# Attention of the last two batches: fp32 scores in 64x32 tiles, p transposed by VectorE, values in 64x64 tiles

## The chip, the cores and the metric

One core of one Trainium2 chip runs the program. The metric is device time in microseconds (us) of one execution, the median of three: 1250.9 us (1250.06 to 1251.99). The profile shown here is of one more execution of the same program, which took 1250.11 us; the profiled span inside it is 1248.3 us.

Engines: PE is TensorE's matmul (PEld its weight load), DVE is VectorE, ACT is ScalarE, POOL is GpSimd, and SP issues the DMAs.

## The reference, cut to what matters

```python
# q, k, v: (4 batches, 8 heads, 1152, 64), fp32
q_pool = q.reshape(B, H, S // 2, 2, D).mean(axis=3)             # 576 queries
scores = scale * np.matmul(q_pool, k.transpose(0, 1, 3, 2))     # 576 x 1152
scores = scores - np.max(scores, axis=-1, keepdims=True)
attn = np.exp(scores)
attn = attn / (np.sum(attn, axis=-1, keepdims=True) + 1e-09)
x = np.matmul(attn, v)                 # heads side by side: 2304 tokens x 512
h = x @ w_in                           # 512 -> 2048
x = np.maximum(0.01 * h, h) @ w_out    # 2048 -> 512
h = np.maximum(np.maximum(x @ w1, x @ w2), x @ w3)   # 512 -> 768, three times
out = h @ w_out2                       # 768 -> 512
```

The two heads of a pair are worked on together: 4 batches of 4 pairs, numbered n = 0 to 15. The third batch begins with pair 8.

## The kernel before

**Two streams.** `attention()` walks over the 16 pairs, and `experts(b)` over the two MoE layers of one batch of tokens. MoE of batch b runs beside the attention of batch b+1; MoE of the last batch runs alone, together with a leftover (`Rest`) of 64 tokens of every batch, 256 in all. Beside the attention of pairs 8 to 15 stands thus the MoE of the second and third batches.

**MoE.** A product (`product`, L706) is 12 matmuls of 128x512 into one PSUM bank, in fp32r (each operand is split in a high and a low part, three matmuls per product of parts). ScalarE or VectorE then take the bank's content away. The last layer (tiles `o`) has 18 matmuls of 128x256 per bank.

**Attention.** A pair goes through two phases, ph 0 with 320 queries and ph 1 with 256. For each query tile:
- `scores` (L318): 128 queries of one head by 1152 keys. Queries and keys are split in a high and a low half that lie on the 128 partitions, so six fp32r matmuls of 128x384 (two per bank, three banks) do a tile; the tile "m" holds the last 64 queries of both heads and takes twelve. That is 36 + 24 = 60 matmuls for a pair. The three banks are one tile `s`, held once: the next tile's matmuls wait until it has been read.
- VectorE takes the row maximum `mx` of the whole tile (L362), ScalarE the exponential into `p` with the row sum beside it (L363).
- `normalise` (L368): from pair 8 on VectorE adds 1e-9, takes the reciprocal and multiplies all of `p` with it (L377, L378, L382).
- `probs_t` and `probs_m` (L407, L418): TensorE transposes `p` in blocks of 128x128 into `pst` and `psf`, 72 + 9 blocks for a pair; ScalarE and VectorE copy them to `pt` (L416, L423).
- `values` (L429): 18 fp32 products a phase, with 64 columns of v as weights and 320 or 256 queries streamed, the two heads in two halves of the columns of the array. `evac` (L452) writes the two parts of x.
- `prep_q`, `prep_k`: transposes of q and k for the next pair, and their split in two halves by ScalarE and VectorE; the halves are sent to the other partitions by DMA (L288).

**PSUM.** From pair 4 on `s` has three banks, `pv` one, and the other four are shared by MoE's products and all transposes (`bank`, L136).

**Order of the work.** The two generators are interleaved by slots (`S_AT`, `RATIO`, L1173), which gives an order to start from. Then `plan()` rebuilds the whole program as a graph, gives each instruction a cost and plays the five engines forward, always taking the step that can start first (ties by how late it may be done); three rounds at most. The order that comes out is fixed for each engine. So an engine never overtakes: if the instruction at its front waits, all behind it wait too.

Of the kernel before, what the change touches and what calls it, by code (L numbers as in the profile page):

```python
# [23 lines left out]
def kernel(  # L24
# [32 lines left out]
    SC = 3  # L57
# [11 lines left out]
    slots = {}  # L69

# [17 lines left out]
    kt_p = Pool("kt", 1)  # L88
    vs_p = Pool("vs", 2)
    p_p = Pool("p", 9)  # L90
    st_p = Pool("st", 12)
    rr_p = Pool("rr", 6)
    m_p = Pool("mb", 1)
    xf_p = Pool("xf", 1)
    pt_p = Pool("pt", 2)
# [8 lines left out]
    ps_v = Pool("ps_v", 1, space=bass.MemoryType.PSUM)  # L104
    ps_m = Pool("ps_m", 2, space=bass.MemoryType.PSUM)
    psum = ExitStack()
    ctx.callback(psum.close)
    ps_5 = Pool("ps_5", 1, psum, space=bass.MemoryType.PSUM)
    s_pair = [ps_5.tile([128, 2, 512], F32, name=f"s2{i}") for i in range(2)]
    s_mid = ps_5.tile([128, 512], F32, name="s1")  # L110

    ident = const.tile([128, 128], F32, name="ident")
    rb = [const.tile([128, w], F32, name=f"rb{w}") for w in (X0, T - X0)]
    qt = {}
    for j in range(2):
        for part in range(2):
            qt[j, part] = const.tile([128, T + 64], F32R, name=f"q{j}{part}")
# [15 lines left out]
    ps_w = {}  # L133
    turn = [0]

    def bank(name, spare=False):  # L136
        if spare:
            return ps_v.tile([128, 512], F32, tag="v", name=name)
        turn[0] += 1
        pool = ps_w["m"] if ps_w and turn[0] % 2 == 0 else ps_m  # L140
        return pool.tile([128, 512], F32, tag="m", name=name)

    def wide_scores():
        if not ps_w:
            psum.close()
            ps_s = Pool("ps_s", 1, space=bass.MemoryType.PSUM)
            ps_w["s"] = ps_s.tile([128, SC, 512], F32, name="s")
            ps_w["m"] = Pool("ps_n", 2, space=bass.MemoryType.PSUM)
        return ps_w["s"]
# [320 lines left out]

    GATE = 0
# [11 lines left out]
    def attention():  # L483
        npair = B * NP
# [31 lines left out]
        for u, (n, ph) in enumerate(phases):  # L516
# [11 lines left out]
            if ph == 0 and n + 1 < npair:  # L528
# [6 lines left out]
                if n + 2 < npair:  # L535
                    at(max(0, s0 + (-2 if early else 15)), 0, load_pair, n + 2)
                if n + 1 >= NP:
                    at(s0 + 8, 0, load_v, n + 1)
            if n < FREE:
# [46 lines left out]
        yield from follow()  # L586
        assert not todo
# [152 lines left out]
    class Rest:  # L740
        n = TR_

        def __init__(self):
            def parts(name):
                t = p_p.tile([128, SC, SN], F32, tag="p", name=name).rearrange("p a b -> p (a b)")
                t = t[:, 0:1024].bitcast(F32R).rearrange("p (i a t) -> p i a t", i=2, a=2)
# [5 lines left out]
            acc = p_p.tile([128, SC, SN], F32, tag="p", name="accrest").rearrange("p a b -> p (a b)")  # L752
# [96 lines left out]
    def plan():  # L849
# [38 lines left out]
        for i in todo:  # L888
# [4 lines left out]
            if key is not None and last and last["unit"] == (key, out):  # L893
# [32 lines left out]
        wide_at = next(n for n, node in enumerate(nodes) if node["out"] and slots[node["out"]][0][0] == "ps_s")  # L926
        for n, node in enumerate(nodes):
            busy = late = move = 0.0
            for i in node["ins"]:
# [4 lines left out]
                if e == "PE":  # L934
                    if kind == "pv":
                        one = cols / 1.2
                    elif kind in ("pst", "psf", "psk", "psr"):
# [14 lines left out]
                elif e == "Activation":  # L952
                    late = 185 + 0.8 * cols + 190 * (len(i.outs) > 1) + 180 * ((kind[0] == "q") or kind == "kspare")
                    busy = late - 105
                elif e == "DVE":
# [3 lines left out]
                    slow = psum or op in ("TensorTensor", "TensorReduce") or kind == "wmant"  # L959
                    late = max(155, 110 + (1.13 if slow else 0.62) * cols + 190 * (kind[0] == "q"))  # L960
                    busy = late - 80
                else:
                    late = 45 + 2.44 * cols
                    busy = late - 45
# [4 lines left out]
            node["busy"], node["late"], node["move"] = busy, late, move  # L969

# [26 lines left out]
        wide = [n for t in users if slots[t][0][0] == "ps_5" for n in users[t]]  # L997
# [7 lines left out]
        def forward(prio):  # L1005
            heads = {g: 0 for g in queue}
            rooms = {g: [(0.0, "")] * slots[q[0]][1] for g, q in queue.items()}
            narrow, narrow_at = len(wide), 0.0
# [10 lines left out]
            values_last = False  # L1019
            for _ in range(count):  # L1020
                best = None
                for e in ENGINES:
                    for n in pool[e]:
                        t = max(ready[n], free[e])
                        if nodes[n]["shut"]:
                            t = max(t, shut)
                        for x in need[n]:
                            group = slots[x][0]
                            if queue[group][heads[group]] != x or not rooms[group]:
                                break  # L1030
                            t = max(t, rooms[group][0][0])
# [179 lines left out]
```

## Time and profile before

| what | value |
|---|---|
| time, median of 3 | 1250.9 us (1250.06 to 1251.99) |
| profiled execution | 1250.11 us, its span 1248.3 us |
| PE busy | 1220.3 us, 98% of the span |
| DVE / ACT / POOL busy | 635.2 / 631.6 / 295.2 us |
| mean granted TensorE clock | 0.996 of full speed |
| second and third batch of MoE beside the attention of pairs 8 to 15 | 460 us to 995 us |
| last batch of MoE, alone | 995 us to the end |

"Busy" is the time in which an engine has an instruction running. PE's instructions overlap: a matmul's record begins when it is issued and ends when its last result has arrived, so the mean duration of one is longer than the pace at which they follow each other. A pace is read from the timeline, as the distance of two starts divided by the number of matmuls between them.

An fp32 product with both operands as they are (here those of `values`) appears in the trace as two matmul records, each with its own weight load; 18 products are 36 records. A transpose and an fp32r matmul are one record each.

### The profile page before, as it was taken

What the parts mean: (1) busy time and instruction counts of PE and PEld (TensorE: products, weight loads), DVE (VectorE), ACT (ScalarE), POOL (GpSimd) and SP (SyncE); (2) the same over time, 40 slices, a digit from 0 to 9 for tenths busy, and PEclk for the clock granted to TensorE, in tenths of its full rate; (3) what the DMA queues carried; (4) which work ended last, traced back from release to release, by engine and by line L of the source; (5) the groups of instructions that cost most, each with busy time, mean ns of one, the idle gap of its engine ahead of it and who ended that gap; (6) DMA issues with size and microseconds to landing.
All of it is one profiled execution on the core that took longest, in us unless ns stands there. A gap on an engine that the chain in (4) does not pass through costs nothing.

```text
span 1248.3 us, 19152 instructions
## 1 busy us (share of the span) xinstructions
PE 1220.3 (98%) x7392; PEld 1006.8 (81%) x7392; DVE 635.2 (51%) x1100; ACT 631.6 (51%) x1251; POOL 295.2 (24%) x265
## 2 busy tenths in 40 slices
PE   6999999999999999999999999999999999999998
PEld 5676677888778887878888897878878798888888
DVE  6877657766776745465655435565645111222110
ACT  6887878676776645453645435453634222112111
POOL 1111144444543412120211101120200022223110
PEclk9999999999999999999999999999999999999999
DMA  5522168676877655363534455363433363333433
GB/s 161 139 74 75 35 223 266 221 231 240 268 252 230 213 166 159 110 175 102 165 130 140 153 184 146 109 190 102 140 122 112 110 206 122 132 120 109 143 110 111
DMA packets 86902, 193.29 MB, mean 155 GB/s; under 512 B 11292, under 2 KB 41756, under 8 KB 86812
## 3 DMA queue, kind: packets, MB, share of 16 engines
q1 hardware_dynamic: 86812, 192.08, 49.1%
q8 instruction: 58, 0.95, 0.3%
q14 instruction: 32, 0.26, 0.1%
HBM read 146.80 MB, written 35.13 MB: 146 GB/s over the span
## 4 chain that ended last, share of the span: by engine, by line
PE 91%; ACT 4%; DVE 3%; issue 1%; DMA 1%; DVEq 0%; ACTq 0%
PE m L123 48%; PE s L123 13%; PE pv L123 11%; PE pst L123 10%; PE o L123 6%; PE psf L123 1%; PE psq L123 1%; PE psk L123 1%; ACT q L280 1%; DVE q L284 1%; DVE kt L233 1%; ACT kt L230 0%; ACT p L358 0%; ACT p L355 0%; ACT p L363 0%
## 5 line engine op out<-in xcount | busy, mean ns | idle before, releaser
L123 PE MATMUL m<-x,w 128*128 128x512 f32 x1224 | 307.2, 396 | 0.3 <-ACT ptw L416 0.3
L123 PEld LDWEIGHTS m<-x,w 128*128 128x128 f32 x1224 | 223.0, 188 | 42.7 <-issue 1.0
L362 DVE TENSOR_REDUCE mx<-s 128x1 f32<-128x1152 f32 x108 | 146.5, 1356 | 105.4 <-PE s L123 105.1
L123 PE MATMUL s<-kt,q 128*128 128x384 f32 x832 | 184.4, 354 | 5.5 <-ACT p L355 2.4
L363 ACT ACTIVATE p<-s,mx 128x1152 f32<-128x1152 f32 x108 | 132.1, 1223 | 93.7 <-DVE mx L362 93.2
L787 POOL TENSOR_TENSOR g<-t,g 128x512 fp32r<-128x512 f32 x64 | 84.1, 1315 | 382.8 <-DVE g L786 382.8
L123 PE MATMUL pst<-ident,p 128*128 128x128 f32 x1080 | 166.4, 276 | 5.1 <-ACT pt L416 1.1
L123 PEld LDWEIGHTS pst<-ident,p 128*128 128x128 f32 x1080 | 129.0, 140 | 49.5 <-issue 11.8
L416 ACT COPY pt<-pst 128x512 f32<-128x512 f32 x216 | 124.6, 587 | 82.6 <-PE pst L123 78.9
L123 PEld LDWEIGHTS s<-kt,q 128*128 128x128 f32 x832 | 143.4, 192 | 14.3 <-ACT p L355 3.1
L123 PE MATMUL m<-g,w 128*128 128x512 f32 x576 | 147.7, 397 | 0.1
L123 PEld LDWEIGHTS m<-g,w 128*128 128x128 f32 x576 | 104.3, 188 | 18.6 <-ACT ptw L416 0.3
L785 ACT ACTIVATE t<-m 128x512 f32<-128x512 f32 x80 | 44.4, 555 | 127.7 <-PE m L123 127.1
L123 PE MATMUL m<-x,wsplit 128*128 128x512 f32 x408 | 106.9, 401 | 0.0
L123 PE MATMUL pv<-pt,v 128*64 128x256 f32 (+1 forms) x720 | 96.7, 407 | 0.0
L665 POOL TENSOR_TENSOR wsplit<-wraw,wsplit 128x512 fp32r<-128x512 f32 x56 | 74.9, 1341 | 83.8 <-ACT wsplit L664 67.0
L815 DVE TENSOR_TENSOR t<-m,t 128x512 f32<-128x512 f32 (+1 forms) x60 | 38.2, 636 | 99.6 <-PE m L123 99.3
L123 PEld LDWEIGHTS m<-x,wsplit 128*128 128x128 f32 x408 | 73.6, 188 | 14.0 <-issue 1.3
L786 DVE CAST g<-t 128x512 fp32r<-128x512 f32 x64 | 27.9, 436 | 107.3 <-ACT t L785 106.9
L123 PEld LDWEIGHTS pv<-pt,v 128*64 128x64 f32 x720 | 48.5, 137 | 37.4 <-issue 8.8
L725 POOL TENSOR_TENSOR y<-t,y 128x512 fp32r<-128x512 f32 x24 | 32.6, 1357 | 187.5 <-ACT y L724 187.5
L382 DVE TENSOR_SCALAR p<-p,sums 128x1152 f32<-128x1152 f32 x76 | 67.2, 885 | 2.6
(120 smaller groups left out, 1577.5 us busy)
## 6 DMA issues: line engine op xcount, KB each, us to landing
w<-w SPq DMA_DIRECT2D x168, 512.0 KB, 3.4
w<-wsplit SPq DMA_DIRECT2D x56, 512.0 KB, 6.5
wraw<-in_moe_w_out_dram SPq DMA_DIRECT2D x22, 512.0 KB, 6.0
wraw<-in_moe_w_dram SPq DMA_DIRECT2D x18, 512.0 KB, 5.1
kraw<-in_k_dram SPq DMA_DIRECT2D x15, 576.0 KB, 9.6
qraw<-in_q_dram SPq DMA_DIRECT2D x15, 576.0 KB
q<-q SPq DMA_DIRECT2D x52, 160.0 KB, 5.2
wraw<-in_moe_w_in_dram SPq DMA_DIRECT2D x16, 512.0 KB, 4.3
```

What stands on the lines that cost most here:

```text
L123: mm = f(*args, **kwargs)
L233: nc.vector.tensor_tensor(out=t[lo, c], in0=src, in1=t[hi, c], op=ALU.subtract)
L362: nc.vector.tensor_reduce(out=mx[:, 0:1], in_=ps[:, :, 0:SN], axis=AX.XY, op=ALU.max, negate=True)
L363: nc.scalar.activation(out=p[2], in_=ps[:, :, 0:SN], func=ACTF.Exp, bias=mx[:, 0:1], accum_out=rs[:, i:i + 1])
L382: nc.vector.tensor_scalar(out=x, in0=x, scalar1=rs[:, i:i + 1], scalar2=None, op0=ALU.mult)
L416: nc.scalar.copy(out=dst, in_=ps.rearrange("p (j c) -> p j c", j=2))
L665: nc.gpsimd.tensor_tensor(out=t[:, 1], in0=r, in1=t[:, 0], op=ALU.subtract)
L725: nc.gpsimd.tensor_tensor(out=t[:, 1], in0=src, in1=t[:, 0], op=ALU.subtract)
L785: nc.scalar.activation(out=t, in_=ps[:, 0:k.n], func=ACTF.Prelu, alpha=0.01)
L786: nc.vector.tensor_copy(out=gt[:, 0], in_=t)
L787: nc.gpsimd.tensor_tensor(out=gt[:, 1], in0=t, in1=gt[:, 0], op=ALU.subtract)
L815: nc.vector.tensor_tensor(out=t, in0=ps[:, 0:k.n], in1=t, op=ALU.max)
```

## The change

Pairs 0 to 7 are left as they were. For pairs 8 to 15 `attention2()` takes over from `attention()`:

- **PSUM.** When the second batch's attention is done, its pools are closed. Attention gets six banks of its own: four for `s` (one tile, held once) and one each for `a` and `b`. MoE keeps two (`ps_m`), where it shared four before.
- **Scores.** `prep2` puts the 64 components of head 0 on partitions 0 to 63 and those of head 1 on 64 to 127, unsplit fp32; no halves, no DMA. `scores2` does 64 queries of both heads in 16 fp32 products of 288 keys, each with 64 rows and 32 columns of the array: two row halves (heads) by four column quarters. A quarter holds 32 queries and half of the keys, so a query's keys lie on two partition groups. A pair has 5 + 4 such tiles.
- **Maximum.** One reduction over the whole tile, then `meet_halves`: four copies of 32 partitions that lay the other half's maximum beside each partition's own, and a minimum (the values are negated).
- **Exponential** in two instructions of 576 elements, one for each head.
- **Transpose.** VectorE's transpose of 32x32 blocks, one instruction for the whole of `p` (128x1152), into `pt`.
- **Values.** `values2` does 72 products a phase with 64 rows and 64 columns of the array (two key halves by two heads); `join` adds the two halves of the row sums by one small product, GpSimd lays their reciprocals out (`rd`), and two products with a constant 0.5 spread them over the partitions. `evac2` multiplies with them, so that `p` itself is not normalised.
- The planner knows the new forms, and some of its other costs are changed (GpSimd's and VectorE's), so the order of the first two batches can move as well.

```diff
+    def split_array():
+        if not sec:
+            full.close()
+            for name, bufs in (("kt", 2), ("vs", 1), ("p", 3), ("rr", 3), ("r", 1), ("pt", 1), ("c", 1), ("rz", 1)):
+                sec[name] = Pool(f"{name}2", bufs)
+            sec["s"] = Pool("ps_q", 1, space=bass.MemoryType.PSUM)
+            sec["v"] = Pool("ps_w", 1, space=bass.MemoryType.PSUM)
...
-        pool = ps_w["m"] if ps_w and turn[0] % 2 == 0 else ps_m
+        pool = ps_w["m"] if ps_w and turn[0] % 2 == 0 and not sec else ps_m
...
+    def other(x, name):
+        return sec["v"].tile([128, 512], F32, tag=x, name=name)
...
-        npair = B * NP
+        npair = NB * NP
...
+    def prep2(n, j):
+        if j == 0:
+            kts2[n] = sec["kt"].tile([128, S], F32, tag="k", name="kt")
+            qts[n] = sec["kt"].tile([128, T], F32, tag="q", name="q")
+        qr = raws[n][0][:, j].rearrange("p c r d -> p (c r d)")
+        kr = raws[n][1][:, j].rearrange("p c d -> p (c d)")
+        r = slice(64 * j, 64 * j + 64)
+        ni = QC // 2
+        w = ni * QP
+        psq, psk = other("a", "psq"), other("b", "psk")
+        for i in range(ni):
+            transpose(psq[:, i * QP:(i + 1) * QP], qr[:, (4 * i + 1) * D:(4 * i + 3) * D], ident[:QP, :QP])
+        transpose(psq[:64, w:w + 128], kr[:, (KT - 1) * D:KT * D], sec["pairs"])
+        for e in range(2):
+            nc.scalar.mul(
+                out=qts[n][r].rearrange("p (t i e) -> p e i t", e=2, i=ni)[:, e],
+                in_=psq[64 * e:64 * e + 64, 0:w].rearrange("p (i t) -> p i t", t=QP),
+                mul=scale,
+            )
+        nc.scalar.copy(
+            out=keys(kts2[n], r, KT - 1, KT),
+            in_=psq[:64, w:w + 128].rearrange("d (m a i) -> d m a i", m=1, a=4),
+        )
+        unit[0] += 1
+        for i in range(4):
+            transpose(psk[:, i * 128:(i + 1) * 128], kr[:, i * 128:(i + 1) * 128], sec["pairs"])
+        unit[0] += 1
+        for e in range(2):
+            nc.scalar.copy(
+                out=keys(kts2[n], r, e, KT - 1, 2),
+                in_=psk[64 * e:64 * e + 64].rearrange("d (m a i) -> d m a i", m=4, a=4),
+            )
...
+    def meet_halves(st, z):
+        for c in range(4):
+            d = c + 1 - 2 * (c % 2)
+            nc.vector.tensor_copy(out=st[32 * c:32 * c + 32, :, 1], in_=st[32 * d:32 * d + 32, :, 0])
+        nc.vector.tensor_reduce(out=z, in_=st, axis=AX.X, op=ALU.min)
+
+    def scores2(n, ph, i):
+        if i == 0:
+            sums2[n, ph] = sec["rr"].tile([128, 2, tiles2(ph)], F32, tag=f"rr{ph}", name="sums")
+            ptl2[n, ph] = flipped(ph)
+        rs, pt = sums2[n, ph], ptl2[n, ph]
+        whole = sec["s"].tile([128, 4, 512], F32, tag="s", name="s")
+        ps = whole
+        every = ps[:, :, 0:KQ].rearrange("p (h x) k -> p h x k", h=2)
+        ps = [ps[:, 0:2], ps[:, 2:4]]
+        c0 = X0 * ph + QB * i
+        unit[0] += 1
+        joint.add(unit[0])
+        for x in range(2):
+            for a in range(4):
+                for h in range(2):
+                    r = slice(64 * h, 64 * h + 64)
+                    c = c0 + 32 * (a // 2)
+                    k0 = KQ * (2 * (a % 2) + x)
+                    matmul(
+                        out=ps[h][32 * a:32 * a + 32, x, 0:KQ],
+                        lhsT=qts[n][r, c:c + 32],
+                        rhs=kts2[n][r, k0:k0 + KQ],
+                        start=True,
+                        stop=True,
+                    )
+        p = sec["p"].tile([128, 4, KQ], F32, tag="p", name="p")
+        st = whole[:, 0, KQ:KQ + 4].rearrange("p (h s) -> p h s", h=2)
+        z = st_p.tile([128, 2], F32, tag="z", name="z")
+        nc.vector.tensor_reduce(out=st[:, :, 0], in_=every, axis=AX.XY, op=ALU.max, negate=True)
+        meet_halves(st, z)
+        for h in range(2):
+            nc.scalar.activation(
+                out=p[:, 2 * h:2 * h + 2], in_=ps[h][:, :, 0:KQ], func=ACTF.Exp, bias=z[:, h:h + 1],
+                accum_out=rs[:, h, i:i + 1],
+            )
+        nc.vector.transpose(
+            out=pt[:, :, i].rearrange("p m h j -> p h m j"),
+            in_=p.rearrange("p (h x) (m i) -> p h (x m) i", h=2, m=KT),
+        )
...
+    def values2(n, ph):
+        w = width2(ph)
+        rs = sums2.pop((n, ph)).rearrange("p h u -> p (h u)")
+        pt = ptl2.pop((n, ph))
+        nu = rs.shape[1]
+        ps = other("b", "psr")
+        unit[0] += 1
+        matmul(out=ps[:, 0:nu], lhsT=sec["join"], rhs=rs, start=True, stop=True)
+        nc.vector.tensor_scalar(out=rs, in0=ps[:, 0:nu], scalar1=1e-9, scalar2=None, op0=ALU.add)
+        nc.vector.reciprocal(out=rs, in_=rs)
+        rd = sec["r"].tile([128, 2 * X0], F32, tag="r", name="rd")[:, 0:2 * w]
+        nj = 2 * w // nu
+        nc.gpsimd.tensor_tensor(
+            out=rd.rearrange("p (u j) -> p u j", j=nj),
+            in0=rs.unsqueeze(2).to_broadcast([128, nu, nj]),
+            in1=sec["fold"].unsqueeze(1).to_broadcast([128, nu, nj]),
+            op=ALU.mult,
+        )
+        unit[0] += 1
+        joint.add(unit[0])
+        two = [other(x, "pw") for x in "ab"]
+        pv2[0] = [two[g][:, 0:w // 2] for g in range(2)]
+        for m in range(2 * KT):
+            for j in range(2):
+                for g in range(2):
+                    r = slice(64 * g, 64 * g + 64)
+                    mm = matmul(
+                        out=pv2[0][g][64 * j:64 * j + 64],
+                        lhsT=vss[n][r, j, m],
+                        rhs=pt[r, m, :, j],
+                        start=(m == 0),
+                        stop=(m == 2 * KT - 1),
+                    )
+        unit[0] += 1
+        pv2[1] = two[0][:, X0 // 2:X0 // 2 + w]
+        for j in range(2):
+            matmul(
+                out=pv2[1][64 * j:64 * j + 64, 0:w],
+                lhsT=sec["half"],
+                rhs=rd[:, j * w:(j + 1) * w],
+                start=True,
+                stop=True,
+            )
+        unit[0] += 1
...
+        nc.scalar.copy(out=rz[:, 0:w], in_=pv2[1][:, 0:w])
+        for g in range(2):
+            a, b_ = [y[:, 0:w].rearrange("p (t g j) -> p g t j", g=2, j=32)[:, g] for y in (xf, rz)]
+            nc.vector.tensor_tensor(out=a, in0=pv2[0][g].rearrange("p (t j) -> p t j", j=32), in1=b_, op=ALU.mult)
+        nc.scalar.copy(out=t[:, 0, c], in_=xf[:, 0:w])
+        nc.gpsimd.tensor_tensor(out=t[:, 1, c], in0=xf[:, 0:w], in1=t[:, 0, c], op=ALU.subtract)
...
+    S2 = ((0, 2, 4, 6, 7), (0, 2, 4, 6))
+    RATIO2 = 1.7
...
+                for i in range(tiles2(nxt[1])):
+                    at(s0 + S2[nxt[1]][i], S_COST, scores2, *nxt, i)
...
+        def both():
+            yield from attention()
+            yield from attention2()
```

The order of the instructions, engine by engine, shows what the planner makes of it. On PE, beside the MoE of the second batch (`m<-x`, `m<-g` are MoE's products), a stretch of the kernel before:

```order
L123 MATMUL m<-g,w 128x512 x18
L123 MATMUL pst<-ident,p 128x128 x4
L123 MATMUL psf<-ident,p 128x128 x3
L123 MATMUL s<-kt_4951,q_123 128x384
L123 MATMUL s<-kt_4951,q_124 128x384
L123 MATMUL s<-kt_4951,q_123 128x384
L123 MATMUL s<-kt_4951,q_124 128x384
L123 MATMUL s<-kt_4951,q_123 128x384
L123 MATMUL s<-kt_4951,q_124 128x384
L123 MATMUL m<-g,w 128x512 x9
L123 MATMUL pst<-ident,p 128x128 x4
L123 MATMUL m<-g,w 128x512 x6
```

The same place now:

```order
L136 MATMUL s<-kt,q 32x288 x16
L136 MATMUL m<-g,w 128x512 x12
L136 MATMUL m<-x,w 128x512 x3
L136 MATMUL s<-kt,q 32x288 x16
L136 MATMUL m<-x,w 128x512 x15
L136 MATMUL s<-kt,q 32x288 x16
L136 MATMUL psr<-sums,join 128x10
L136 MATMUL m<-x,w 128x512 x9
L136 MATMUL pw<-pt,v 64x160 x72
L136 MATMUL pw<-rd,half 64x320 x2
L136 MATMUL m<-x,w 128x512 x3
L136 MATMUL s<-kt,q 32x288 x16
```

The groups of four transposes (`pst`) and of three (`psf`) are gone, and the six fp32r matmuls of a score tile have become one block of 16; most often 18 matmuls of MoE stand between two score tiles (29 times of 71). The phase's values come as one block of 72 and, a little later, two products of `rd`.

On DVE, in the same stage, before:

```order
L362 TENSOR_REDUCE mx<-s 128x1
L799 TENSOR_TENSOR acc<-m,acc 128x512
L377 TENSOR_SCALAR sums<-sums 128x1
L378 RECIPROCAL sums<-sums 128x1
L382 TENSOR_SCALAR p<-p,sums 128x1152
L423 COPY pt<-psf 128x6x64
```

and now (`s<-s` with four copies is the meeting of the halves, `z` the maximum):

```order
L705 TENSOR_REDUCE s<-s 128x2
L674 COPY s<-s 32x2 x4
L675 TENSOR_REDUCE z<-s 128x2
L712 STREAM_TRANSPOSE pt<-p 128x2x18x32
L1058 CAST g<-t 128x512
L705 TENSOR_REDUCE s<-s 128x2
L674 COPY s<-s 32x2 x4
L675 TENSOR_REDUCE z<-s 128x2
L1058 CAST g<-t 128x512
L712 STREAM_TRANSPOSE pt<-p 128x2x18x32
```

The reciprocal and the multiplication of `p` have left the tile's chain, and the copies, the second minimum and the transpose have come into it; the transpose stands ahead of the next tile's reduction or of a step of MoE.

On PE, where the attention of the last batch ends and MoE's last batch begins, before:

```order
L123 MATMUL pst<-ident,p 128x128 x8
L123 MATMUL pv<-ptw,v 64x320 x6
L123 MATMUL pv<-pt,v 64x320 x6
L123 MATMUL pv<-ptw,v 64x320 x6
L123 MATMUL pst<-ident,p 128x128 x24
L123 MATMUL o<-w,y 128x256 x15
L123 MATMUL pv<-pt,v 64x256 x6
L123 MATMUL pv<-ptw,v 64x256 x6
L123 MATMUL pv<-pt,v 64x256 x6
L123 MATMUL o<-w,y 128x256 x129
L123 MATMUL m<-x,w 128x512 x12
L123 MATMUL m<-xrest,w 128x256 x12
```

and now:

```order
L136 MATMUL s<-kt,q 32x288 x16
L136 MATMUL o<-w,y 128x256 x30
L136 MATMUL s<-kt,q 32x288 x16
L136 MATMUL o<-w,y 128x256 x30
L136 MATMUL s<-kt,q 32x288 x16
L136 MATMUL o<-w,y 128x256 x30
L136 MATMUL psr<-sums,join 128x10
L136 MATMUL s<-kt,q 32x288 x16
L136 MATMUL o<-w,y 128x256 x3
L136 MATMUL pw<-pt,v 64x160 x72
L136 MATMUL pw<-rd,half 64x320 x2
L136 MATMUL s<-kt,q 32x288 x16
```

Before, the last values stood ahead of 129 matmuls of the last MoE layer; now the last score tiles stand among them, 30 matmuls apart.

## Rows read from the trace of the kernel before

**Rows 1.** The page, busy time of each engine over the span.
```profile
PE 1220.3 (98%) x7392; PEld 1006.8 (81%) x7392; DVE 635.2 (51%) x1100; ACT 631.6 (51%) x1251; POOL 295.2 (24%) x265
```

**Rows 2.** The page, the chain that ended last, share by engine.
```profile
PE 91%; ACT 4%; DVE 3%; issue 1%; DMA 1%; DVEq 0%; ACTq 0%
```

**Rows 3.** Windows, pairs 8 to 15: stretch, length, busy time and count each, clock.
```profile
460.00:995.00 535.00, 532.55 (x3154) 436.37 (x3153) 277.72 (x486) 253.32 (x473) 84.59 (x65) 1.00 0.46 140
```

**Rows 4.** Timeline of PE: start, length of the group, operation, count.
```profile
502.84 0.60 PE L123 MATMUL pst<-ident,p 128*128 128x128 f32 x4
503.20 2.32 PE L123 MATMUL m<-x,w 128*128 128x512 f32 x9
505.35 0.60 PE L123 MATMUL pst<-ident,p 128*128 128x128 f32 x4
505.71 1.31 PE L123 MATMUL s<-kt,q 128*128 128x384 f32 x6
506.85 1.55 PE L123 MATMUL m<-x,w 128*128 128x512 f32 x6
508.24 0.60 PE L123 MATMUL pst<-ident,p 128*128 128x128 f32 x4
```

**Rows 5.** Timeline of PE, values and transposes of the last pair.
```profile
980.01 1.83 PE L123 MATMUL pv<-ptw,v 128*64 128x320 f32 x12
...
985.01 2.84 PE L123 MATMUL pst<-ident,p 128*128 128x128 f32 x24
987.61 2.03 PE L123 MATMUL o<-w,y 128*128 128x256 f32 x15
989.57 1.52 PE L123 MATMUL pv<-pt,v 128*64 128x256 f32 x12
...
993.60 6.62 PE L123 MATMUL o<-w,y 128*128 128x256 f32 x53
```

**Rows 6.** Timeline of PE in stretches of 5 ns: what runs there.
```profile
980.34 0.44 PE L123 MATMUL pv<-ptw,v 128*64 128x320 f32 x2
...
980.60 0.44 PE L123 MATMUL pv<-ptw,v 128*64 128x320 f32 x2
```

**Rows 7.** Timeline of all engines, one score tile from its start to the next.
```profile
645.42 1.00 PEld L123 LDWEIGHTS s<-kt,q 128*128 128x128 f32 x6
...
646.78 1.36 DVE L362 TENSOR_REDUCE mx<-s 128x1 f32<-128x1152 f32 x1 [0.74 <-PE s L123]
...
648.17 1.22 ACT L363 ACTIVATE p<-s,mx 128x1152 f32<-128x1152 f32 x1 [1.80 <-DVE mx L362]
...
649.29 0.19 ACT L363 ACTIVATION_READ_ACCUMULATOR p<-s,mx 128x1 f32 x1
...
649.57 2.18 PEld L123 LDWEIGHTS s<-kt,q 128*128 128x128 f32 x12
```

**Rows 8.** Groups by line: count, busy us, mean ns, idle before and releaser.
```profile
L416 ACT COPY pt<-pst 128x512 f32<-128x512 f32 x216 | 124.6, 587 | 82.6 <-PE pst L123 78.9 <-PE pv L123 2.6
...
L382 DVE TENSOR_SCALAR p<-p,sums 128x1152 f32<-128x1152 f32 x76 | 67.2, 885 | 2.6
...
L815 DVE TENSOR_TENSOR t<-m,t 128x512 f32<-128x512 f32 x48 | 33.1, 689 | 80.4 <-PE m L123 80.1
...
L358 ACT ACTIVATE p<-s,mx 128x768 f32<-128x768 f32 x24 | 21.7, 905 | 0.0
...
L355 ACT ACTIVATE p<-s,mx 128x384 f32<-128x384 f32 x21 | 12.4, 588 | 4.1 <-DVE mx L354 4.0
...
L354 DVE TENSOR_REDUCE mx<-mx 128x1 f32<-128x2 f32 x36 | 5.6, 154 | 1.2
```

**Rows 9.** Timeline of PE, products of the last MoE batch and of the leftover.
```profile
1050.98 2.91 PE L123 MATMUL m<-x,w 128*128 128x512 f32 x12
1053.73 1.59 PE L123 MATMUL m<-xrest,w 128*128 128x256 f32 x12
1055.16 2.91 PE L123 MATMUL m<-x,w 128*128 128x512 f32 x12
```

More of the change, by code (lines that the diff above doesn't have):

```diff
@@ L586, in attention, with load_v2, keys @@
         yield from follow()
+        assert not todo
+    kts2 = {}
+    qts = {}
+    def load_v2(n):
+        b, hp = divmod(n, NP)
+        h0 = 2 * hp
+        vss[n] = sec["vs"].tile([128, 2, 2 * KT, D], F32, tag="v", name="v")
+        for g in range(2):
+            nc.sync.dma_start(
+                out=vss[n][64 * g:64 * g + 64], in_=v[b, h0:h0 + 2].rearrange("h (p c) d -> p h c d", p=64)
+            )
+    def keys(t, r, m0, m1, step=1):
+        return t[r].rearrange("d (a m i) -> d m a i", a=4, m=KT)[:, m0:m1:step]
@@ L892, in plan @@
             last = nodes[-1] if nodes else None
-            if key is not None and last and last["unit"] == (key, out):
+            if key is not None and last and (last["unit"] == (key, out) or key in joint and last["unit"] and last["unit"][0] == key):
                 last["ins"].append(i)
@@ L924, in plan @@
             before[node_of[a]].add(node_of[b])
-        wide_at = next(n for n, node in enumerate(nodes) if node["out"] and slots[node["out"]][0][0] == "ps_s")
+        wide_at = next(
+            n for n, node in enumerate(nodes) if node["out"] and slots[node["out"]][0][0] in ("ps_s", "ps_q")
+        )
         for n, node in enumerate(nodes):
@@ L934, in plan @@
                 if e == "PE":
[L935 removed]
+                    if kind == "pv" or kind == "pw" and cols >= X0 - 64:
                         one = cols / 1.2
+                    elif kind == "pw":
+                        one = cols / 2.4
+                    elif kind == "s" and cols == KQ:
+                        one = cols / 4.8
                     elif kind in ("pst", "psf", "psk", "psr"):
@@ L969, in plan @@
             node["busy"], node["late"], node["move"] = busy, late, move
+            kind = node["out"].rsplit("_", 1)[0] if node["out"] else ""
+            node["mode"] = {"pv": 1, "psz": 1, "pw": 3}.get(kind, 2 * (kind == "s" and cols == KQ))
         after = [[] for _ in nodes]
@@ L1060, in forward @@
                     group = slots[x][0]
+                    if group[0] in ENTER and not heads[group]:
+                        held[n].extend(leaving[ENTER[group[0]]])
                     heads[group] += 1
                     held[n].append(heappop(rooms[group])[1])
-                    if group[0] in ("ps_s", "ps_n"):
-                        held[n].extend(t for t in users if slots[t][0][0] == "ps_5")
                 for x in node["tiles"]:
@@ L1156, in advance @@
                 spent[1] += d
-        for c in attention():
+        def both():
+            yield from attention()
+            yield from attention2()
+        for c in both():
             if c == "room":
```

184 lines of the change are left out of this document (146 added, 38 removed).

## The prediction

> **What bounds the kernel now.** I read the page's busy times first: PE is busy for 1220.3 us, 98% of the span, and no other engine for more than 51% [rows 1]. The chain that ended last says the same: 91% of it is PE, ScalarE and VectorE have 7% together [rows 2]. Then the stretch that the change touches, from MoE's second batch to the end of attention: of 535 us PE is busy for 532.6, at the full clock (1.00, its level of 2.4 GHz), VectorE for 277.7, ScalarE for 253.3, GpSimd for 84.6 [rows 3]. So in this stretch what PE no longer does comes off the time, nearly all of it, as long as the other engines don't begin to make PE wait. The last views are PE's timeline, for the pace of each kind of work [rows 4 to 6, 9], and one score tile followed through all engines [rows 7].
>
> **The change part by part.** Counts are those of the eight pairs 8 to 15, read from the code and the order; all of it is PE time on the path unless said otherwise.
>
> Transposes: 8 x (72 + 9) = 648 blocks go. 24 of them in a row take 987.61 - 985.01 = 2.60 us [rows 5], 0.108 each; a group of four among other work takes 0.36 us to the next start and delays what follows by some 0.1 [rows 4], so about the same. 648 x 0.108 = -70.0 us. With them go 144 copies of ScalarE at 587 ns and the multiplication of p on VectorE, 72 x 885 ns [rows 8]; neither engine is on the path, and I count nothing for them.
>
> Scores: 8 x 60 = 480 matmuls go. Six take 506.85 - 505.71 = 1.14 us [rows 4], 0.19 each: -91.2 us. In come 72 blocks of 16 products, 32 records. No row has a tile of 64 by 32, so its price has to be bounded. In the values, two tiles of 64 columns work side by side: two records run in each slot, and slots follow each other by 980.60 - 980.34 = 0.26 to 0.27 us for 320 columns [rows 6], or 0.83 ns a column. A slot of 288 columns is then 0.24 us. If all eight tiles run side by side, 32 records are 4 slots, 0.96 us. If only the four column quarters do (the rows show concurrency between column tiles alone), it is 8 slots, 1.92 us. Changing the array's division costs something too: the phase's values are 18 slots, 4.81 us, and take 985.01 - 980.01 = 5.00 [rows 5], 0.19 over; the work after such a block adds a little, and I take 0.3 for a block with its way in and out. I take eight side by side, since the pair of records in [rows 6] starts together, so that a second tile waits neither for the issue nor for the end of the first: 72 x (0.96 + 0.3) = +90.7. The two forms of the scores cost the same.
>
> On this the Trainium skill has a rule that speaks against the change: a switch of the tiling mode drains the array ("TensorEngine Tiling (Array Packing)", Tiling Modes, Key Properties). The trace agrees that a switch has a price, 0.19 us in [rows 5]; by the rule alone, without a size for it, nothing could be added, and with no price for it the sum would be 88 x 0.3 = 26 us lower.
>
> Values: before, 8 x (5.00 + 4.03) = -72.2 us (993.60 - 989.57 = 4.03 for the phase of 256 queries [rows 5]). Now 72 products, 144 records, over four tiles are 36 slots: of 160 columns 36 x 0.133 = 4.80 us, of 128 columns 36 x 0.107 = 3.84. With 0.3 a block: 8 x (8.64 + 0.6) = +73.9. If the two row halves don't run side by side this doubles, +69 more. The price of not normalising p is the two products of rd, 2 slots of 0.267 or of 0.213: 8 x 0.96 = +7.7, and 16 small products for the sums, some 0.1 each, +1.6. GpSimd's rd is covered by the block of values in front of its products; the transposes for q and k stay as many.
>
> Waits: the new risk. The score tile is held once, before and now, so between two tiles stands a chain through three engines. Before it is 649.57 - 645.42 = 4.15 us [rows 7]: PE to the reduction 1.36, reduction to exponential 1.39, exponential to the next weights 1.40. Now the first part is about 1.4. The second has four copies and a minimum more; the nearest row, the minimum over 128x2, takes 154 ns [rows 8], so 0.77 at most in sequence, 0.4 if they overlap by half. The third is two exponentials of 576 elements; between 588 ns for 384 and 905 for 768 [rows 8] lies 746, so 1.49 and a last read of 0.19 [rows 7], 1.7 with the hand-over. Sum 4.9 to 5.3 us, plus what VectorE has in front of a reduction. That is above all the transpose of p: bounded below by the 0.82 to 0.89 us of a multiplication of the same 1152 elements [rows 8], above by twice the reduction's 1.36 [rows 7]. It starts when the exponentials end, and the next reduction comes 1.4 us later, so at 1.3 us (the value I take, the reduction's) it only just fits, and a step of MoE behind it (689 ns [rows 8]) makes the reduction late. I take 5.4 us for the chain.
>
> Against it stands what PE has to do from one score tile to the next. At the paces above, with MoE at 0.229 us (2.75 for 12 [rows 9]), the most frequent distance, 18 matmuls and the block of 1.26, is 5.4 us. Over the 71 distances of the order, 9 are under 5.0 us, 38 between 5.0 and 5.5, and 24 longer. With a chain of 5.4, adding up what is missing in the short ones gives 8 us of waiting: +8.
>
> The sum: -70.0 - 91.2 + 90.7 - 72.2 + 73.9 + 7.7 + 1.6 + 8 = -51.5 us. From the profiled execution's 1250.1 us that is 1198.6; the median of the runs is 0.8 us above that execution, so I say 1199.
>
> **What costs nothing, and its cover.** Attention of pair 8 begins later than before, behind the closing of the old pools; 72 matmuls of the last layer and 30 of MoE's next batch stand there for PE. VectorE gets 72 transposes (94 us at 1.3), the copies and minima (at most 55) and loses 64 us of multiplication and the low halves of q and k; some 320 us of a stretch of 485 is no bound, but it is where the waits come from. MoE has two banks instead of four: a bank is read for about 0.9 us (689 ns and the hand-overs) while the other takes 12 matmuls, 2.75 us, or 1.43 for the leftover [rows 9], so nothing as long as the reading engine is free.
>
> **The rivals.**
>
> *The row halves don't work side by side (slower).* No row shows two tiles on different partition halves at work. If they take turns, the score blocks cost 72 x 0.96 = 69 us more and the values 69 more, and the chain is 1 us longer while PE's work between tiles grows by as much. 1199 + 138 = 1337. It decides as soon as more than a third of this is real, since 51 us are to be lost. Against it: tiles on different columns overlap fully [rows 6].
>
> *They overlap in part.* A third lost on both forms, by gaps between weight loads and streams of so many short records: 72 x 0.29 + 69 x 0.3 = +42, 1241. The Trainium skill measures less than the ideal: 10.6 times for 16 tiles ("TensorE: Matmul & The Clock Gate", Part 3, Measured speedup vs the span model); taken for both forms, 0.66 of the ideal, its figure would give an estimate of 1270. No run here shows it.
>
> *The chain is longer.* 47 of the 71 distances are under 5.5 us, so each 0.1 us beyond costs 4.7 us. A transpose near its upper bound, or VectorE and ScalarE with steps of MoE ahead of the tile's, makes 6.2 us and 44 us of waiting in place of 8: 1235. At 6.5 us nothing is left of the gain, and beyond it the kernel is slower. For it: PE's order is fixed, so a late tile stops MoE behind it. The Trainium skill warns of this, that after tiling the emptying of PSUM may become the bound ("TensorEngine Tiling (Array Packing)", Performance Considerations, PSUM Bottleneck); before, VectorE still sat idle for 0.74 us ahead of the reduction [rows 7].
>
> *Two banks are too few.* An engine that reads a MoE bank behind an exponential pair (1.7 us) or a reduction comes late; at 0.3 us for some 80 products, 1223.
>
> **How the numbers follow.** A measurement of this kernel can tell about 0.2% (2.5 us) from no change. Forecast 1199: 0.54, its own range 1182 to 1215 (chain 4.9 to 5.7, switch 0.2 to 0.4). Partial overlap, 1241: 0.07. Longer chain, around 1235: 0.15 still faster, 0.03 no change, 0.04 slower. Two banks, 1223: 0.03. Row halves in turn, 1337: 0.14. Faster is 0.54 + 0.07 + 0.15 + 0.03 = 0.79, the same 0.03, slower 0.18. The range goes from 1180 (switches and chain at their cheap ends) to 1262, past the chain's break-even; what lies outside is above all the row halves in turn.
>
> **What would show it.** Groups of score blocks at 16 products in about 1.3 us from their start to what follows, and values blocks of 72 in about 5.1 and 4.1 us, show the tiles side by side; 2.2 us and 9.6 us show turns. The distance of two reductions near 5.4 us, with PE idle in front of a score block for less than 0.2 us on average, shows the chain; idle time there released by ScalarE's exponential shows it too long. PE idle in front of MoE products, released by ScalarE or VectorE, shows the banks. Attention should end about 50 us sooner, and MoE's last batch take its 253 us as before. The prediction is wrong if the time is above 1250, or if it falls by 51 us while the score blocks take another time than 1.3 us.

## The result, and the profile after

The changed kernel takes 1219.86 us (median of 4 runs, 1217.47 to 1221.03) against 1250.48 us of the kernel before: a ratio of 0.9751, interval 0.9731 to 0.9770. It is faster by 31 us, inside the range, and 21 us short of the gain that was forecast.

Busy time of each engine over the span of 1219.2 us, to be held against [rows 1]:

```profile
PE 1177.4 (97%) x10392; PEld 924.0 (76%) x10392; DVE 655.2 (54%) x1229; ACT 577.7 (47%) x1235; POOL 328.1 (27%) x305
```

PE does less, by 42.9 us, and is still the bound; but the span fell by 1248.3 - 1219.2 = 29.1 us only, so PE is idle for 13.8 us more. The stage from MoE's second batch to the start of its last shows where most of this is; the columns are those of [rows 3]. First the kernel before, from its first such matmul to the one of the last batch:

```profile
460.19:1009.18 548.99, 546.54 (x3272) 450.36 (x3270) 277.72 (x486) 255.26 (x479) 84.59 (x65) 1.00 0.46 141
```

and the changed kernel, between the same two matmuls:

```profile
453.61:980.81 527.20, 513.24 (x6338) 379.72 (x6337) 313.01 (x646) 214.53 (x488) 114.99 (x97) 1.00 0.50 154
```

Before, PE is idle in this stage for 548.99 - 546.54 = 2.5 us, now for 527.20 - 513.24 = 14.0, 11.5 more. The clock is at its full level in both. Ahead of the stage 6.6 us are gained, in MoE's last batch 0.7; the stage is 21.8 us shorter.

PE's timeline in this stage, to be read like [rows 4] (in brackets the idle time ahead and what ended it):

```profile
469.30 1.20 PE L136 MATMUL s<-kt,q 64*32 64x288 f32 x32
470.43 4.39 PE L136 MATMUL m<-g,w 128*128 128x512 f32 x18
475.63 1.20 PE L136 MATMUL s<-kt,q 64*32 64x288 f32 x32 [0.81 <-ACT p L708]
476.76 4.38 PE L136 MATMUL m<-g,w 128*128 128x512 f32 x18
481.07 1.20 PE L136 MATMUL s<-kt,q 64*32 64x288 f32 x32
...
495.62 5.12 PE L136 MATMUL pw<-pt,v 64*64 64x160 f32 x144
500.67 0.76 PE L136 MATMUL pw<-rd,half 128*64 128x320 f32 x4
501.36 0.97 PE L136 MATMUL m<-x,w 128*128 128x512 f32 x3
```

A score block takes 470.43 - 469.30 = 1.13 us to the start of the next work, a phase's values 500.67 - 495.62 = 5.05: all eight, and all four, tiles work side by side. Between two score blocks stand 18 MoE matmuls, and one block of the three waits 0.81 us for ScalarE's exponential. One score tile through the engines shows what it waits for, as [rows 7] did before:

```profile
486.52 0.67 PEld L136 LDWEIGHTS s<-kt,q 64*32 64x32 f32 x32 [1.05 <-ACT p L708]
...
487.92 1.37 DVE L705 TENSOR_REDUCE s<-s 128x2 f32<-128x1152 f32 x1
489.32 0.78 DVE L674 COPY s<-s 32x2 f32<-32x2 f32 x4
490.13 0.16 DVE L675 TENSOR_REDUCE z<-s 128x2 f32<-128x4 f32 x1
490.41 0.74 ACT L708 ACTIVATE p<-s,z 128x576 f32<-128x576 f32 x1 [3.46 <-DVE z L675]
...
491.14 0.73 ACT L708 ACTIVATE p<-s,z 128x576 f32<-128x576 f32 x1
491.76 0.20 ACT L708 ACTIVATION_READ_ACCUMULATOR p<-s,z 128x1 f32 x1
...
492.00 1.38 DVE L712 STREAM_TRANSPOSE pt<-p 128x1152 f32<-128x1152 f32 x1 [1.71 <-ACT p L708]
492.01 0.67 PEld L136 LDWEIGHTS s<-kt,q 64*32 64x32 f32 x32 [1.08 <-ACT p L708]
```

From weights to weights it takes 492.01 - 486.52 = 5.49 us, where it was 4.15: 1.40 to the reduction, 2.49 from there to the exponential, 1.60 to the next tile. The four copies have 0.78 us. Along this chain PE, DVE and ACT take turns: each starts when the one before it has ended.

A second wait shows only inside a block. Where the next pair's first block starts, PE gets 2 of its 32 records out and stops:

```profile
655.64 0.67 PE L136 MATMUL s<-kt,q 64*32 64x288 f32 x2
656.67 1.20 PE L136 MATMUL s<-kt,q 64*32 64x288 f32 x30 [0.36 <-ACT kt L652]
```

Those 30 wait for ScalarE's copies of that pair's keys, which stand behind an exponential and the copies of the queries in its queue (the exponential's last read, then `q`, then `kt`):

```profile
653.59 0.20 ACT L708 ACTIVATION_READ_ACCUMULATOR p<-s,z 128x1 f32 x1
653.81 1.46 ACT L638 ACTIVATE q<-psq 64x288 f32<-64x288 f32 x2
655.28 0.26 ACT L643 COPY kt<-psq 64x128 f32<-64x128 f32 x1
655.45 1.17 ACT L652 COPY kt<-psk 64x512 f32<-64x512 f32 x2
```

The bracket says 0.36 us, since the two records are counted as 0.67 of work; by the starts the block loses more. Six blocks are longer than the usual 1.13 us by 0.28, 0.72, 1.03, 1.35, 1.24 and 1.13 us, 5.75 together.

### The profile page after: what moved, and what is told of

It is laid out like the page before. It is cut to its first block, busy times and chain, and to the rows that moved or that the text cites. A ratio compares the mean times of both kernels' runs of the same rounds, so it can differ in the third digit from the quotient of the medians.

```text
span 1219.2 us, 25415 instructions
## 1 busy us (share of the span) xinstructions
PE 1177.4 (97%) x10392; PEld 924.0 (76%) x10392; DVE 655.2 (54%) x1229; ACT 577.7 (47%) x1235; POOL 328.1 (27%) x305
## 5 line engine op out<-in xcount | busy, mean ns | idle before, releaser
L136 PE MATMUL s<-kt,q 64*32 64x288 f32 (+1 forms) x2656 | 172.4, 403 | 16.7 <-ACT p L708 9.3
L708 ACT ACTIVATE p<-s,z 128x576 f32<-128x576 f32 x144 | 105.6, 738 | 173.8 <-DVE z L675 171.9
L712 DVE STREAM_TRANSPOSE pt<-p 128x1152 f32<-128x1152 f32 x72 | 99.3, 1379 | 104.5 <-ACT p L708 104.5
L136 PEld LDWEIGHTS s<-kt,q 64*32 64x32 f32 (+1 forms) x2656 | 97.3, 118 | 63.0 <-ACT p L708 25.1
L705 DVE TENSOR_REDUCE s<-s 128x2 f32<-128x1152 f32 x72 | 98.4, 1367 | 24.8 <-PE s L136 22.8
L136 PE MATMUL pst<-ident,p 128*128 128x128 f32 x504 | 80.1, 278 | 2.1 <-DVE kspare L250 0.7
L136 PEld LDWEIGHTS pst<-ident,p 128*128 128x128 f32 x504 | 59.1, 140 | 25.9 <-issue 6.7
L136 PEld LDWEIGHTS m<-pt,w 128*128 128x128 f32 x600 | 75.4, 188 | 4.3 <-ACT t L1057 0.7
L136 PE MATMUL m<-pt,w 128*128 128x256 f32 x600 | 76.6, 279 | 0.8 <-ACT t L1057 0.5
L136 PE MATMUL pw<-pt,v 64*64 64x160 f32 (+1 forms) x2304 | 74.3, 284 | 0.0
```

Source lines behind the costliest of these rows:

```text
L136: mm = f(*args, **kwargs)
L705: nc.vector.tensor_reduce(out=st[:, :, 0], in_=every, axis=AX.XY, op=ALU.max, negate=True)
L708: nc.scalar.activation(out=p[:, 2 * h:2 * h + 2], in_=ps[h][:, :, 0:KQ], func=ACTF.Exp, bias=z[:, h:h + 1], accum_out=rs[:, h, i:i + 1],)
L712: nc.vector.transpose(out=pt[:, :, i].rearrange("p m h j -> p h m j"), in_=p.rearrange("p (h x) (m i) -> p h (x m) i", h=2, m=KT),)
```

## The experiments

The theory at this point: the transposes' PE time came off, and what it gained was given back in part to the chain of a score tile, in part to the products for the denominators. In the code cuts "..." marks what is left out. Times are medians, with the ratio to the kernel before and its interval.

**The transposes alone, on the kernel before.**

```diff
-            probs_t(n, ph, gr * PG + g)
+            if n < 2 * NP or gr == 0:
+                probs_t(n, ph, gr * PG + g)
...
-            pt = pts.pop((n, ph, gr))
+            pt = pts[n, ph, 0 if n >= 2 * NP else gr]
```

> The kernel before, in which pairs 8 to 15 transpose only the first third of p on TensorE and use it three times over (left out: two thirds of the transposes and their copies; the result is not the reference's). Theory: PE's time is the bound, so 432 blocks at 0.108 us with what they delay come off whole: -47 us, about 1204 (1198 to 1210). Rival: the score chain or the readers set the pace there, and less than half comes off: above 1227.

Measured: 1198.69 us, 0.9587 (0.9571 to 0.9603), 52 us less than before. The stage, from MoE's second batch to the start of its last:

```profile
463.78:961.21 497.43, 497.38 (x2839) 407.26 (x2838) 266.58 (x470) 204.28 (x383) 84.70 (x65) 1.00 0.50 156
```

PE has almost no idle time left in the stage (0.05 us). 432 blocks brought 52 us, 0.12 us each, a tenth more than the 0.108 of the theory; 2.4 of the 52 are idle time that PE had in this stage before (2.5 us). The rival, that something else sets the pace before, is out.

**The chain shorter and longer.** The first kernel leaves out the meeting of the halves, the second does its copies twice.

```diff
-        nc.vector.tensor_reduce(out=st[:, :, 0], in_=every, axis=AX.XY, op=ALU.max, negate=True)
-        meet_halves(st, z)
+        nc.vector.tensor_reduce(out=z, in_=every, axis=AX.XY, op=ALU.max, negate=True)
```

> The changed kernel without the four copies and the minimum in the chain of a score tile; each partition keeps its own half's maximum (left out: the meeting of the halves; the result is not the reference's). The chain is 1.0 us shorter, 4.5 instead of 5.49. Theory: what was lost beyond the blocks is waiting on this chain, 10 us in front of score blocks and 6 behind: -8 to -14 us, 1206 to 1212. Rival: the loss is in PE's own way in and out of the blocks, or the planner puts the work as tightly round the shorter chain: within 3 us of 1219.

```diff
-        for c in range(4):
+        for c in [*range(4)] * 2:
```

> The changed kernel with each of the four copies done twice, the same result: the chain is 0.78 us longer, 6.27. Theory: the planner knows of only a part of it and PE waits at the 40 or so tiles that stand close: +20 to +37 us, 1239 to 1256. Rival: there is room enough between tiles (7.3 us on average), so waits move rather than grow: +0 to +8 us.

Measured: 1205.05 us, 0.9634 (0.9619 to 0.9648), and 1248.83 us, 0.9988 (0.9977 to 0.9998). The same stage in the kernel without the meeting:

```profile
452.35:964.05 511.70, 509.23 (x6339) 379.64 (x6337) 252.39 (x286) 214.48 (x488) 114.76 (x97) 1.00 0.51 159
```

and in the one that meets twice:

```profile
452.50:1007.63 555.13, 517.77 (x6338) 379.67 (x6337) 358.78 (x934) 212.43 (x488) 114.53 (x97) 1.00 0.47 146
```

PE has the same matmuls in all three. Its idle time is 2.5 us without the meeting, 14.0 with it, 37.4 with it twice; the time moves by 14.8 us down and 29.0 up. So the whole step of 1.1 us of chain is paid (medians of the 72 tiles: without the meeting the exponential starts 1.45 us after the reduction for 2.49, and the reduction 0.08 us sooner), and another 0.78 us eats nearly all that the change had gained, though the starts of two tiles are 7.1 us apart on average. The planner packs them close: between two tiles stand most often 18 MoE matmuls (29 times of 71); without the meeting it is 15 (26 times), so the order follows the shorter chain, and with the meeting twice still 18 (26 times), so it does not follow the longer one. The long distances elsewhere are no help.

**The order of the products within a block.** Two kernels with the same 16 products in another order: the two of one tile directly behind each other, and all eight of one head ahead of the other's.

```diff
-        for x in range(2):
-            for a in range(4):
-                for h in range(2):
+        for a in range(4):
+            for h in range(2):
+                for x in range(2):
```

> The changed kernel with the two products of one 64x32 tile directly behind each other, in place of one round over all eight tiles and then another; same result. Theory: the tiles overlap because PE gets them in turn; a product whose tile is busy stops those behind it, the block grows from 1.13 us to 2 to 4 us and the time by 60 to 200 us. Rival: PE looks past a waiting product, the block stays at 1.13 us and the time within 3 us of 1219.

```diff
-        for x in range(2):
-            for a in range(4):
-                for h in range(2):
+        for h in range(2):
+            for x in range(2):
+                for a in range(4):
```

> The changed kernel with all eight products of one head (one row half of the array) ahead of the eight of the other; same result. Theory: PE takes products past one whose tile is busy, as with the same tile in a row, so the block stays between 1.13 and 1.25 us and the time within 9 us of 1219. Rival: with the halves apart only four tiles work at a time, the block is 2.1 us and the time 70 us longer.

Measured: 1226.63 us, 0.9806 (0.9786 to 0.9825), and 1223.47 us, 0.9786 (0.9768 to 0.9803). PE's timeline with the same tile in a row:

```profile
482.54 1.25 PE L136 MATMUL s<-kt,q 64*32 64x288 f32 x32
483.72 3.01 PE L136 MATMUL m<-g,w 128*128 128x512 f32 x12
```

and with one half first:

```profile
487.76 1.24 PE L136 MATMUL s<-kt,q 64*32 64x288 f32 x32 [0.63 <-ACT p L708]
488.92 3.69 PE L136 MATMUL m<-x,w 128*128 128x512 f32 x15
```

The block becomes 1.18 and 1.16 us for 1.13. My theory of the first, that a product with a busy tile stops those behind it and makes the block 2 to 4 us, has fallen: the tiles overlap in all three orders. Its rival has the block nearly right and the time not: 6.8 us over the changed kernel (3.6 with one half first), where the blocks explain about 4 (and 2); the rest is open. The theory of the second, 1.13 to 1.25 us a block and within 9 us, holds.

**A cheaper meeting.** Each query needs one shift for all of its keys, not the maximum.

```diff
-        nc.vector.tensor_reduce(out=st[:, :, 0], in_=every, axis=AX.XY, op=ALU.max, negate=True)
-        meet_halves(st, z)
+        nc.vector.tensor_reduce(out=z, in_=every, axis=AX.XY, op=ALU.max, negate=True)
+        for c in (1, 3):
+            nc.vector.tensor_copy(out=z[32 * c:32 * c + 32], in_=z[32 * c - 32:32 * c])
```

> The changed kernel, in which both key halves of a query use the first half's maximum: the reduction writes it, two copies of 32 partitions carry it over, no minimum (any shift gives the same softmax as long as nothing overflows). The chain of a score tile is some 0.6 us shorter, about 4.9. Theory: the time follows the chain's length at the slope seen between the chains of 4.5, 5.49 and 6.27 us, 15 us for the first and 29 for the second step: -8 to -12 us, 1208 to 1212. Rival: only the whole meeting's removal pays, since the planner spaces tiles in steps of three MoE matmuls (0.69 us): above 1216.

Measured: 1211.84 us, 0.9691 (0.9677 to 0.9706), as the slope says for a chain that is 0.65 us shorter (the exponential 1.92 us after the reduction, the reduction 0.08 sooner). Not all of it arrives: to the first matmul of MoE's last batch the stage is 16.7 us shorter, and from there to the end it takes 8.7 longer. 4.7 of these are the last values, which stand behind that matmul now; the batch waits for what comes of them:

```profile
967.42 4.16 PE L136 MATMUL pw<-pt,v 64*64 64x128 f32 x144
...
972.09 0.97 PE L136 MATMUL m<-pt,w 128*128 128x256 f32 x6
973.66 1.31 PE L136 MATMUL m<-x,w 128*128 128x512 f32 x3 [0.60 <-ACT x L778]
975.66 4.61 PE L136 MATMUL m<-x,w 128*128 128x512 f32 x12 [0.69 <-ACT t L1058]
```

Behind these two waits the granted clock falls: 12 such matmuls take 4.61 us here for the usual 2.9. Windows of 5 us there (0.66 is the mean of a stretch partly at 1.2 GHz):

```profile
970.00:975.00 5.00, 4.29 (x73) 2.78 (x65) 0.49 (x2) 0.78 (x2) 0.73 (x1) 1.00 0.02 3
975.00:980.00 5.00, 4.34 (x12) 3.42 (x13) 0.43 (x1) 0.60 (x1) 1.28 (x1) 0.66 0.26 66
```

**Attention sooner.** `RATIO2 = 1.5` for 1.7.

> The changed kernel with RATIO2 1.5 for 1.7: less of MoE is put beside each step of attention, so that attention ends before MoE's last layer runs out, where the tiles now stand 30 small matmuls apart. Theory: this takes away the 4.5 us of waits among those matmuls and no others: 1214 to 1219. Rival: the planner's passes undo the order it is given, so nothing changes: within 2 us of 1220.

Measured: 1216.73 us, 0.9737 (0.9723 to 0.9752); the interval overlaps with that of the changed kernel, so the 3 us are not settled.

**From the second batch, and from the fourth.** `NB = 1` and `NB = 3` for 2 (`NB` counts the batches from 0, so these are the second and the fourth).

> The changed kernel with the new attention from the second batch on (pairs 4 to 15, NB = 1), beside the MoE batch whose weights are split on the fly. Theory: there VectorE has the decoding of weights too (about 87 us) and with 36 tiles at about 3.9 us it becomes the bound of that batch, near 255 us; PE's saving of up to 25 us is lost for the most part: 1210 to 1225, with PE idle behind VectorE in that batch. Rival: PE stays the bound and a third batch gains what each of the other two did, 15 us: about 1205. Other rival: VectorE's queue makes it slower than 1225.

> The changed kernel with the new attention for the last batch alone (pairs 12 to 15, NB = 3). Theory: each batch gains by itself, half of 31 us: 1233 to 1238. Rival: most of the gain, or of the loss, is at one place (the hand-over of the pools, or the last batch beside the leftover): outside 1229 to 1242.

Measured: 1202.00 us, 0.9616 (0.9601 to 0.9630), and 1237.82 us, 0.9899 (0.9882 to 0.9915). The last batch alone gives 13 us, the third with it 31, the second with both 48. The first part of the second batch's stage with NB = 1:

```profile
150.00:300.00 150.00, 143.80 (x1541) 101.45 (x1545) 119.84 (x230) 102.20 (x207) 81.08 (x69) 1.00 0.81 257
```

VectorE is busy for 119.84 of 150 us, 80%, and PE for 143.80, 96%. From 172 to 440 us PE is idle for 11.8 us, of which 7.6 are in front of score blocks, ended by ScalarE's exponential, and 2.0 ended by VectorE. So PE stays the bound: my theory, which had VectorE full there, was wrong, and the rival with PE as the bound and 15 us a batch came near (18).

**Without the denominators.** `psr`, the reciprocals, `rd` and its two products are left out of `values2`, the multiplication out of `evac2`.

> The changed kernel without the products that bring in the row sums (psr, the reciprocals, rd and its two products; left out: the division, so the result is not the reference's). Theory: 14.3 us of PE between the starts of these products and of what follows them, and the waits behind score blocks for psr with them: -13 to -18 us, 1202 to 1207. Rival: the prediction's own term, -9 us: about 1211.

Measured: 1207.48 us, 0.9656 (0.9643 to 0.9669): they cost 12.4 us, just short of what the theory gave and more than the 9 of the prediction. With the products went what the other engines do for them, so the 12.4 are not PE's alone.

**ScalarE's preparation sooner.** The copies of the next pair's keys and queries get earlier slots.

```diff
-    PREP2 = (5, 7)
+    PREP2 = (2, 4)
```

> The changed kernel with one pair of numbers other: the copies by which ScalarE prepares the next pair's keys and queries stand three slots earlier in its queue. Theory (the rest of the miss is 5.7 us of waits inside six score blocks, where TensorE has issued 2 of 32 records and waits for ScalarE's copy of the next pair's keys, which stands behind exponentials): those waits go, 4 to 6 us are gained, 1214 to 1216 us. Rival (the copies only push exponentials back, and the next product waits for those instead): within 2 us of the changed kernel, 1218 to 1222 us.

Measured: 1217.36 us, 0.9741 (0.9724 to 0.9759), 2.5 us less; the interval overlaps with that of the changed kernel. The waits inside the blocks did go, but for one of 0.85 us: the excess falls from 5.75 us (and one of 0.16) by about 5. The group of all score products, first of the changed kernel, in its stage:

```profile
L136 PE MATMUL s<-kt,q 64*32 64x288 f32 x2304 | 90.3, 409 | 11.5 <-ACT p L708 9.3 <-ACT kt L652 2.1
```

and here:

```profile
L136 PE MATMUL s<-kt,q 64*32 64x288 f32 x2304 | 87.2, 409 | 11.0 <-ACT p L708 10.8 <-ACT kt L652 0.2
```

(the last columns are the idle time and what ended it). What waited for keys now waits in part for exponentials, 10.8 us for 9.3: of 5 us removed the stage keeps 3 (524.1 us for 527.2). Theory and rival each have half of it, and the time is between the two.

**The three that paid, together:** `NB = 1`, two copies, `RATIO2 = 1.5`.

> The three changes that paid, together: the new attention from the second batch on, two copies instead of the meeting, RATIO2 1.5; the result is the reference's. Theory: they act on different waits and add up: 1202 less 12 for the chain of now 108 tiles and 2 for the order: 1186 to 1192. Rival: VectorE bounds the second batch, so a shorter chain does nothing there and the rest only moves waits: 1196 to 1202.

Measured: 1185.27 us, 0.9478 (0.9463 to 0.9493), 35 us faster than the changed kernel and 65 than the one before. One by one they gave 17.9 + 8.0 + 3.1 = 29 us; with the two copies counted for 108 tiles instead of 72 it is 33. So nothing of the gains is lost between them, and the time is just under the theory's range.

## Why the prediction was right in its direction and too large

**What held.** PE was the bound and stayed it. The rival that carried most of the risk, row halves in turn, is excluded by the blocks of 1.13 us, and the partial overlap with it. Values came out at 5.05 and 4.09 us a phase (5.1 and 4.1 were said), 72.2 before against 73.1 now. MoE's last batch takes as long as before. PE never idles ahead of MoE's products in the stage, so two banks are enough. A score chain of 5.4 us was taken; it is 5.49.

**What was luck.** The time lies outside the forecast's own range (1182 to 1215) and inside the whole one, whose upper part stood there for a longer chain (1235) and for too few banks (1223). The second didn't come. Of the first a part of the waits came, and the longer chain didn't. The signs for it could not decide: PE is idle for 0.13 us in front of a score block on average, under the 0.2 that was to show the chain as taken, and ScalarE's exponential ends that wait, which was to show it too long.

**What did not hold: the size of four terms.** The working adds up to -51.5 us, the runs show -30.6.

| step | predicted | measured | how |
|---|---|---|---|
| transposes | -70.0 | about -69 | distances of starts over the timeline, and 84 delays of 0.09 behind them; -78 by the first experiment's 0.12 a block |
| scores | -0.5 | +7 | 72 x (1.13 + 0.09 ahead + 0.11 behind) against 480 x 0.186 |
| values | +1.7 | +1 | 8 x 9.14 against 8 x 9.03 |
| denominators | +9.3 | +12 | left out: -12.4 |
| waits | +8 | +15 | meeting left out: -14.8 |
| first two batches | 0 | +3 | 6.6 us gained there, 10 us of pair 8's work gone from there |

Two steps failed by 7 us each. The first is the waits, and in it not the chain's length but what was counted: I added what the short distances lack, 8 us. To the 9.3 us in front of score blocks, a little more than that, come the 5.75 inside six of them, for ScalarE's copies of keys, for which the sum had no term. Both hang on the chain: without the meeting the blocks inside lose 0.25 us at most. The second is the scores: the way in and out of a block, 0.3 us where it is 0.37 (1.13 and both sides, less 0.96 of streaming), and the removed scores, whose pace over the whole stage is 0.186 us and not the 0.19 of [rows 4]. The third, by 3 us, is the denominators: the pair of `rd` takes 0.69 us (501.36 - 500.67 above) and 0.58 to the next work, where 0.53 and 0.43 were counted, and the product for the sums 0.24 in 10 of 16 places, where 0.1 was. That the other division of the array (128x64 for `rd`, by the trace) is the reason is not shown. The last row, the planner's new order in the batches that were left alone, I had not priced. By the timeline's figure for the transposes the rows sum to -31, by the first experiment's to -40; in that kernel the reading engines had less to do as well, and 2.4 of its 52 us are PE's idle time, so its 0.12 us are more than PE's share. Between the two 9 us stay unassigned.

The sign "attention ends about 50 us sooner" was wrong: the work behind its last products starts at 980.35 us for 993.60, 13 us sooner, since the order spreads attention to the end of MoE's batch. What moved by the gain is the start of MoE's last batch, 1009.2 to 980.8.

The Trainium skill's page "TensorEngine Tiling (Array Packing)", Performance Considerations, PSUM Bottleneck, was the apter of the two rules: the engines that empty the banks did become what PE waits for, with 9.3 us in front of score blocks, though PE stays the bound. The page's rule that a change of the tiling mode drains the array (Tiling Modes, Key Properties) goes with the 0.37 us a block; that these are a drain no run shows. The 10.6 times for 16 tiles of the Trainium skill's page "TensorE: Matmul & The Clock Gate", Part 3, Measured speedup vs the span model, would by the prediction's estimate have made the streaming of both forms half as long again. The values lose little, 5.05 us for 4.80; a score block takes 1.13 us for 0.96, and 1.33 with both sides.

## What to carry to other kernels

When work leaves the engine that bounds, price next the longest loop through the engines that hold one buffer: here every 0.1 us of it cost 1.2 to 3.7 us, and a cheaper shift (two copies for four and a minimum) was worth a quarter of the whole change. Where a planner packs to a cost that is too short, the misses are paid at each close place, whatever the average distance is: 29 us here for 0.78 us that the order did not follow. And try a change that pays by itself in the places that were left out: from the second batch on it brought 18 us more.

## What the runs showed of the hardware that was not expected

- Fp32 products on eight 64x32 tiles overlap, in each of three orders: 1.13, 1.16 and 1.18 us for 32 records, of which 0.96 is streaming at the pace of [rows 6]; four tiles at a time would be 1.92.
- The first 128x512 matmul behind a block of small tiles takes 0.337 us to the next start, behind transposes 0.314, behind the fp32r scores 0.232, in a row 0.228 (medians or means over the timelines of the two kernels).
- Four copies of 32 partitions by 2 elements take 0.78 us with nothing between them, 0.195 each. VectorE's transpose of 128x1152 takes 1.38 us, as long as the maximum over the same elements (1.37).
